# The end of round 0 spread over three engines in a fused RWKV-6 and MLP kernel

## The chip, the core and the metric

The kernel runs on one core of one Trainium2 chip. The core has TensorE (PE in the profile; its weight loads are listed apart as PEld), VectorE (DVE), ScalarE (ACT), GpSimd (POOL) and SyncE (SP), which here only issues transfers. Each runs its own instruction stream in order, and they meet through semaphores. The metric is the device time of one execution in microseconds (us). Five runs of the kernel before took 597.77, 600.28, 598.0, 605.68 and 603.4 us; their median is 600.28.

## The reference

Two blocks follow each other. The first is a linear attention with a state that decays per step; B, H, S, D are 4, 8, 768, 48:

```python
for t in range(S):
    kt, vt, rt, wt = (k[:, :, t], v[:, :, t], r[:, :, t], w[:, :, t])
    cur = np.einsum('bhd,bhe->bhde', u[None] * kt, vt)
    y[:, :, t] = np.einsum('bhd,bhde->bhe', rt, state + cur)
    state = wt[:, :, :, None] * state + np.einsum('bhd,bhe->bhde', kt, vt)
```

Its output, (4, 768, 8 x 48 = 384), is x for the second, a normalised two-layer MLP with a residual, of inner width 1536:

```python
xn = (x - mu) / np.sqrt(var + 1e-06) * g_ln
ch = np.maximum(xn @ w_ch1, 0.0) @ w_ch2
return (x + ch).astype(np.float32)
```

r, k, v, w and u come as float32. The two MLP weight matrices are float64 in the inputs.

## The kernel before

**Rounds and units.** The sequence of each of the 4 batches is cut into two halves of 384 steps. That makes 8 rounds, and each round has two units of 4 heads (`units`, q in the code; u0 and u1 are those of round 0, `new` those of round 1). A unit's 384 steps are 3 tiles of 128 rows, each of two chunks of 64 steps.

**One round of attention.** `load` brings w, k, r of a unit; `turned` transposes one pair of heads on PE (three 128x128 transposes into one of two PSUM buffers, tag "t") and ScalarE copies it out as wT, rT or kT. Inside a chunk, the scores are built in 6 levels by doubling blocks: `quads` multiplies kT and rT on PE into `a_ps` (one of two PSUM buffers of tag "a"), `grow` multiplies decays into rT and kT in place on VectorE, `keep` copies the level's part of the scores to A under a mask on VectorE. `totals` makes the decay products that the levels need. The last level isn't copied under a mask but as four blocks of 32 rows, together with four copies of rT to the other half of the partitions (`rx`, two per unit); `keep` only lists these eight copies and `finish(n)` does the next n of them, all on ScalarE. `ends` transposes the grown kT back (kn), `states` multiplies kn and v on PE (kv, tag "a") and runs the decayed sum over six chunks on VectorE (s), `exchanged` copies s to the other half of the partitions on ScalarE (sx). `outputs` multiplies A with v and vx (v with its chunk rows exchanged by a DMA) and rT, rx with s, sx into y (tag "a"), and VectorE adds the step's own term. That term, `own_term` (vo), is v times `own`, and `own` in rounds 0 and 1 comes from `products` (r times k on VectorE) and `product_sums` (12 records of own_ps on PE and a copy on ScalarE).

**The MLP of a round.** `moments` and `norm` normalise x (VectorE, one root on ScalarE), `turned_x` transposes it, `mlp` is a generator: 12 steps h (three 128x384 matmuls each, six records, then a copy with a floor at zero on ScalarE), then 12 steps of three matmuls of the second layer (o_ps). Its steps fill PE during the levels of the next round; `UNTIL` says how many steps are done when a level ends.

**Weights.** The float64 weights come in 24 parts of 128x384. `fetch` loads the next raw part (4 buffers, on SP's queue), `begin` splits it into three pieces with three ScalarE instructions and fetches another, `join` puts them together with three VectorE instructions (w_sb). The first 12 parts are the first layer's, the others the second's; from part 16 on a begin needs one of 4 small buffers, which the join four parts back frees. `converted(n)` joins up to part n just before an MLP step that needs it. `BEGINS` and `JOINS` set how many of each stand in the six levels of round 1.

**Order.** `InOrder` wraps every engine, so each engine's stream is the order of the code; the profile puts all its instructions on that wrapper's line 49, and they are told apart by tile names. SP's loads by `SPO` are in that order too. `fill` mixes a level's list of tasks (loads, begins, joins, round 2's transposes in `ahead`) with MLP steps. `warm(n)` puts multiplications of zeros by zeros, n blocks of 128 columns (tile idle), on PE.

**Around the change.** In round 0 there is no MLP yet. Its levels 2 to 5 each run three of the twelve transposes of round 1 (line 691 on). After level 5 come ends, round 1's products, finish, states, outputs, moments, norm and turned_x, and then the loop of rounds 1 to 8 (line 748 on).

Of the kernel before, what the change touches and what calls it, by code (L numbers as in the profile page):

```python
# [9 lines left out]
F32 = mybir.dt.float32  # L10
# [42 lines left out]
def kernel(  # L53
# [59 lines left out]
        for nm in "wkr"  # L113
    }
    vn, vx, xs = {}, {}, {}

    def steps(src, q, c):

# [309 lines left out]
                for j in range(2):  # L428
                    late.append((a["rx"][ds(HP * (1 - j), HP)], R[ds(HP * j, HP), :, 1, :]))

    def finish(n):

        for _ in range(n):
            out_, in_ = late.pop(0)
            ACT.copy(out=out_, in_=in_)

    def ends(q, pr):

# [45 lines left out]
                in_=a["s"].rearrange("p r (c i) e -> p r c i e", i=2)[ds(HP * j, HP), :, :, 0],  # L484
            )

    def outputs(q):
        b, f, g = units[q]
        a = st.pop(q)
        if g == 0:  # L490
            xs[b, f] = p2.tile([P, TT, H, D], F32, tag="x", name=f"x{b}_{f}")
        y = ps_a.tile([P, 2, 512], F32, tag="a", name=f"y{q}")
        y = y[:, :, 0 : NK * D].rearrange("p j (k e) -> p j k e", k=NK)
        A = a_bufs[q // U % 2]
        for k_ in range(NK):
            pr, c = divmod(k_, TT)
            for i in range(2):
                for j in range(2):
                    rows = ds(C * (i ^ j), C)
                    PE.matmul(  # L500
                        y[ds(C * i, C), j, k_], A[rows, j, q % U, k_, :],
                        vx[q][rows, c, pr] if j else vn[q][rows, c, 2 * pr],
                        start=k_ == 0, stop=False, skip_group_check=True,
                    )
# [15 lines left out]
        for j in range(2):  # L520
            DVE.tensor_tensor(
                out=xs[b, f][:, :, ts(g, NH)]
                .rearrange("p c (r j) e -> p j r c e", j=2)[:, j],
                in0=y[:, j].rearrange("p (r c) e -> p r c e", r=NP),
                in1=a["vo"].rearrange("p c (r j) e -> p j r c e", j=2)[:, j], op=ALU.add,
            )
        del vn[q], vx[q]


    xns, xTs, mvs = {}, {}, {}  # L530

    def moments(rnd):
        b, f = rounds[rnd]
        x, name = xs[b, f], f"{b}_{f}"
        stats = p2.tile([P, TT, DVE.BN_STATS_DIM], F32, tag="stats", name=f"stats{name}")
        mv = mvs[rnd] = p2.tile([P, TT, DVE.BN_AGGR_DIM], F32, tag="mv", name=f"mv{name}")
        for i in range(TT):
            DVE.bn_stats(out=stats[:, i, :], in_=x[:, i].rearrange("p h d -> p (h d)"))
        for i in range(TT):
            DVE.bn_aggr(out=mv[:, i, :], in_=stats[:, i, :])  # L540

    def norm(rnd):
        b, f = rounds[rnd]
# [137 lines left out]
    products(u1)  # L681
    quads(u1, 0)
    fetch(2)
    load(new[1], eng=SPO)
    run(each(load_v, [u0, u1], [SPO]) + each(load_vx, [u0, u1], [SPO]))
    begin()
    begin()
    warm(3)
    grow(u1, 0)
    keep(0, 0)  # L690
    ahead = each(turned, new[:1], "wrk", pairs) + each(turned, new[1:], "wrk", pairs)
    for lev in range(1, NLEV):
# [51 lines left out]
    while len(UNTIL) < NR * NLEV:  # L744
        UNTIL.append(UNTIL[-1] + MLP_STEPS // NLEV)
    ahead = [t for nm in "wkr" for t in each(turned, units_of(2), nm, pairs)]
    JOINS, BEGINS = (3, 3, 3, 4, 4, 4), (3, 3, 3, 3, 4, 2)
    for rnd in range(1, NR + 1):
        old, now, new = units_of(rnd - 1), units_of(rnd), units_of(rnd + 1)
        if rnd == 1:  # L750
# [1 line left out]
        for lev in range(NLEV):  # L752
# [123 lines left out]
```

## Time and profile before

| | before |
|---|---|
| median of 5 runs | 600.28 us (597.77 to 605.68) |
| the profiled execution | 597.77 us, its span 596.0 us |
| busy PE / VectorE / ScalarE / GpSimd | 574.5 / 295.1 / 198.1 / 70.6 us |
| mean granted TensorE clock | 0.982 |
| granted clock 42.6 to 59.6 us | 0.50 |
| grow of round 1's level 0 starts (VectorE) | 58.85 us |
| states of round 1 start (VectorE) | 112.52 us |

The span runs from the first to the last instruction of one profiled execution. The page gives each engine's busy time, then the span in 40 slices of 14.9 us with the busy share in tenths; "PEclk" is the share of full speed that TensorE's clock was granted. A busy PE isn't PE at full rate: a matmul's row counts from its issue to its modelled end, and neighbours overlap. A timeline row reads: start, duration, engine, line, operation, output and inputs, shape, count and, in brackets, the idle time before it and who ended it. A row of the chain of work reads: start, length, what.

### The profile page before, as it was taken

To read this page: it belongs to the slowest core of one execution; us is meant where nothing else is said; L and a number is where in the kernel's file an instruction comes from. 1 tells how busy PE (TensorE), PEld (TensorE's weight loads), DVE (VectorE), ACT (ScalarE), POOL (GpSimd) and SP (SyncE) were. 2 spreads that over 40 slices of the span, in tenths; PEclk is the share of its full clock that TensorE was granted. 3 is DMA by queue.
4 is the path that set the end of the run, shared out by engine and by line. 5 is a ranking of instruction groups with operands and counts; after the bars stand their busy time and mean duration, and the time that the engine had idled before them with its cause. 6 is when DMAs were issued, how large, how long until landed. Compare 5 with 4: busy or idle time off the path is not lost.

```text
span 596.0 us, 19117 instructions
## 1 busy us (share of the span) xinstructions
PE 574.5 (96%) x8542; PEld 387.7 (65%) x8542; DVE 295.1 (50%) x706; ACT 198.1 (33%) x430; POOL 70.6 (12%) x100
## 2 busy tenths in 40 slices
PE   8989997999999999999999999999999999999997
PEld 5679665666666666666666666667666666666554
DVE  4876997889365445425265334626245532130000
ACT  3483877503452125211343114321251015301200
POOL 6000000004250025000240007000230000000000
PEclk9995999999999999989999999999999999999999
DMA  9974896045323402222113402012000000000000
GB/s 146 201 187 111 177 252 164 3 89 115 62 43 70 99 15 41 55 58 59 30 26 63 95 14 55 2 32 58 15 2 3 15 25 5 2 14 26 0 14 26
DMA packets 122129, 36.82 MB, mean 62 GB/s; under 512 B 115776, under 2 KB 118976, under 8 KB 122048
## 3 DMA queue, kind: packets, MB, share of 16 engines
q1 hardware_dynamic: 119648, 35.31, 27.1%
q8 instruction: 67, 1.10, 0.8%
q10 hardware_dynamic: 2400, 0.30, 0.5%
q14 instruction: 14, 0.11, 0.1%
HBM read 28.51 MB, written 4.72 MB: 56 GB/s over the span
## 4 chain that ended last, share of the span: by engine, by line
PE 83%; DVE 10%; ACT 3%; issue 2%; POOL 1%; DMA 1%; DVEq 0%; POOLq 0%
PE o_ps L49 29%; PE h_ps L49 28%; PE a_ps L49 10%; PE y L49 4%; DVE w_sb L49 3%; DVE A L49 2%; PE kv L49 2%; PE r_ps L49 2%; PE k_ps L49 2%; DVE rT L49 2%; PE own_ps L49 1%; PE kn_ps L49 1%; PE w_ps L49 1%; PE xT_ps L49 1%; DVE kT L49 1%
## 5 line engine op out<-in xcount | busy, mean ns | idle before, releaser
L49 PE MATMUL o_ps<-w_sb,h 128*128 128x384 f32 x576 | 198.9, 492 | 3.2 <-ACT h L49 3.2
L49 PE MATMUL h_ps<-xT,w_sb 128*128 128x384 f32 x576 | 195.8, 489 | 0.6 <-ACT h L49 0.6
L49 PEld LDWEIGHTS o_ps<-w_sb,h 128*128 128x128 f32 x576 | 105.3, 191 | 65.2 <-ACT h L49 3.8
L49 PEld LDWEIGHTS h_ps<-xT,w_sb 128*128 128x128 f32 x576 | 105.4, 190 | 64.1 <-ACT h L49 0.8
L49 PEld LDWEIGHTS a_ps<-rT,kT 48*64 48x64 f32 x4608 | 74.7, 136 | 21.3 <-issue 13.4
L49 PE MATMUL a_ps<-rT,kT 48*64 48x32 f32 x4608 | 79.9, 221 | 5.8 <-issue 4.8
L49 ACT ACTIVATE h<-h_ps 128x384 f32<-128x384 f32 x96 | 46.5, 488 | 114.5 <-PE h_ps L49 110.2
L49 DVE TENSOR_TENSOR o<-o_ps,x 128x384 f32<-128x384 f32 x24 | 13.4, 558 | 133.1 <-PE o_ps L49 133.0
L49 POOL TENSOR_TENSOR vo<-v,own 128x576 f32<-128x576 f32 x12 | 14.3, 1195 | 363.0 <-DVE own L49 361.5
L49 DVE COPY_PREDICATED A<-mask,a_ps 128x384 f32<-128x384 int8 x80 | 54.6, 753 | 0.0
L49 DVE TENSOR_TENSOR kT<-kT,tot 128x384 f32<-128x384 f32 x80 | 45.5, 569 | 11.1 <-PE a_ps L49 10.3
L49 DVE TENSOR_TENSOR rT<-rT,tot 128x384 f32<-128x384 f32 x80 | 45.7, 580 | 8.7 <-PE a_ps L49 8.7
L49 DVE SCALAR_TENSOR_TENSOR s<-s,decay,kv 128x48 f32<-128x48 f32 x160 | 29.3, 260 | 28.1 <-PE kv L49 28.1
L49 DVE TENSOR_TENSOR x<-y,vo 128x288 f32<-128x288 f32 x32 | 13.2, 454 | 53.7 <-PE y L49 53.7
L49 ACT ACTIVATE xT<-xT_ps,g_sb 128x384 f32<-128x384 f32 x24 | 13.7, 581 | 59.8 <-PE xT_ps L49 59.8
L49 ACT COPY kT<-k_ps 128x384 f32<-128x384 f32 x32 | 14.9, 478 | 40.9 <-PE k_ps L49 40.9
L49 PEld LDWEIGHTS y<-v,A 64*64 64x64 f32 x384 | 22.9, 144 | 8.0 <-issue 6.0
L49 ACT COPY rT<-r_ps 128x384 f32<-128x384 f32 x32 | 14.4, 478 | 39.2 <-PE r_ps L49 39.2
L49 PE MATMUL y<-v,A 64*64 64x48 f32 x384 | 26.2, 232 | 0.8 <-DVE A L49 0.8
L49 PE MATMUL y<-vx,A 64*64 64x48 f32 x384 | 26.1, 232 | 0.0
L49 PE MATMUL y<-sx,rx 48*64 48x48 f32 x384 | 25.4, 229 | 0.0
L49 ACT COPY kn<-kn_ps 128x384 f32<-128x384 f32 x32 | 14.2, 481 | 30.3 <-PE kn_ps L49 30.3
(70 smaller groups left out, 554.0 us busy)
## 6 DMA issues: line engine op xcount, KB each, us to landing
raw<-in_moe_w_ch_dram SPq DMA_DIRECT2D x24, 384.0 KB, 4.3
nat_w<-in_w_dram SPq DMA_DIRECT2D x48, 96.0 KB, 2.8
nat_k<-in_k_dram SPq DMA_DIRECT2D x48, 96.0 KB, 3.0
v<-in_v_dram SPq DMA_DIRECT2D x48, 96.0 KB, 3.2
out_dram<-o SPq DMA_DIRECT2D x24, 192.0 KB, 1.9
nat_r<-in_r_dram SPq DMA_DIRECT2D x45, 96.0 KB, 2.9
vx<-v SPq DMA_DIRECT2D x32, 72.0 KB, 2.3
nat_r<-in_r_dram ACTq DMA_DIRECT2D x3, 96.0 KB, 4.0
```

Of the source, the lines that this page charges most:

```text
L49: return lambda *args, **kw: self.tc.keep_in_program_order(f(*args, **kw))
```

## The change

Four of the eight copies of `finish` go to VectorE and two to GpSimd. Both own terms of round 0 go to GpSimd. The products and sums of round 1's units are moved: those of its first unit between the outputs, those of the second behind them, its sums into round 1's level 0. The last output of round 0 is multiplied tile by tile, and its add on VectorE is split into six, each pair followed by that tile's moments. Round 1's transposes run as 2, 3, 3, 2, 2 in levels 1 to 5 instead of 3 in each of levels 2 to 5. One more begin runs in round 0's levels and one at the end of its tail; two are moved ahead of the loads of k and v. The numbers of warm blocks and the tables of MLP steps, joins and begins change. The diff, cut to its core:

```diff
-    def finish(n):
+    def finish(n, eng=ACT):
         for _ in range(n):
             out_, in_ = late.pop(0)
-            ACT.copy(out=out_, in_=in_)
+            (ACT.copy if eng is ACT else eng.tensor_copy)(out=out_, in_=in_)
...
-    def outputs(q):
+    def outputs(q, by_tile=False):
...
-        for k_ in range(NK):
-            pr, c = divmod(k_, TT)
+        order = [(pr, c) for pr in pairs for c in range(TT)]
+        if by_tile:
+            order.sort(key=lambda at: at[1])
+        for pr, c in order:
+            k_ = pr * TT + c
...
-        for j in range(2):
-            DVE.tensor_tensor(
...
+        for cs in [[c] for c in range(TT)] if by_tile else [range(TT)]:
+            c, n = cs[0], len(cs)
+            for j in range(2):
+                DVE.tensor_tensor(
...
+            if by_tile:
+                moments(q // U, c, 1)
...
-    load(new[1], eng=SPO)
-    run(each(load_v, [u0, u1], [SPO]) + each(load_vx, [u0, u1], [SPO]))
+    load(new[1], "wr", SPO)
     begin()
     begin()
+    load(new[1], "k", SPO)
+    run(each(load_v, [u0, u1], [SPO]) + each(load_vx, [u0, u1], [SPO]))
...
-        if lev > 1:
-            run(ahead[3 * lev - 6 : 3 * lev - 3])
-        if lev in (3, 4):
+        run(ahead[(0, 2, 5, 8, 10)[lev - 1] : (2, 5, 8, 10, 12)[lev - 1]])
+        if 1 < lev < NLEV - 1:
             begin()
-        warm((6, 3, 2, 2, 3)[lev - 1])
+        warm((3, 1, 1, 2, 0)[lev - 1])
...
     run(each(ends, [u0, u1], pairs))
-    for q in new:
-        products(q)
-    finish(6)
-    warm(1)
+    finish(4, DVE)
+    finish(2)
+    finish(2, POOL)
     states(u0)
     exchanged(u0)
-    finish(2)
+    own_term(u0, POOL)
     states(u1)
+    product_sums(u1)
+    own_term(u1, POOL)
     exchanged(u1)
-    product_sums(u1)
     load(units_of(2)[0], "w", SPO)
-    own_term(u0, DVE)
+    warm(2)
+    products(new[0])
+    outputs(u0)
+    warm(3)
     begin()
-    outputs(u0)
-    product_sums(new[0])
-    begin()
-    own_term(u1, DVE)
     join()
-    outputs(u1)
-    product_sums(new[1])
-    moments(0)
+    outputs(u1, by_tile=True)
+    warm(2)
     load(units_of(2)[1], "w", SPO)
     for q in new:
         quads(q, 0)
+    products(new[1])
+    product_sums(new[0])
     norm(0)
     begin()
     join()
     warm(2)
     run(each(turned_x, [0], range(KC)))
+    begin()
     join()
...
-    UNTIL = [3, 6, 8, 11, 14, 16, 19, 21, 24]
+    UNTIL = [4, 7, 10, 12, 14, 16, 19, 21, 24]
...
-    JOINS, BEGINS = (3, 3, 3, 4, 4, 4), (3, 3, 3, 3, 4, 2)
+    JOINS, BEGINS = (3, 3, 4, 4, 4, 3), (3, 3, 3, 4, 4, 2)
...
+                if lev == 0:
+                    tasks += each(product_sums, now[1:])
```

More of the change, by code (lines that the diff above doesn't have):

```diff
@@ L115 @@
     vn, vx, xs = {}, {}, {}
+    xns, xTs, stats, mvs = {}, {}, {}, {}
     def steps(src, q, c):
@@ L502, in outputs @@
                         vx[q][rows, c, pr] if j else vn[q][rows, c, 2 * pr],
-                        start=k_ == 0, stop=False, skip_group_check=True,
+                        start=(pr, c) == order[0], stop=False, skip_group_check=True,
                     )
@@ L519, in outputs, with moments @@
                     )
-        for j in range(2):
-            DVE.tensor_tensor(
[L522 to L526, printed above, removed]
+        for cs in [[c] for c in range(TT)] if by_tile else [range(TT)]:
+            c, n = cs[0], len(cs)
+            for j in range(2):
+                DVE.tensor_tensor(
+                    out=xs[b, f][:, ds(c, n), ts(g, NH)]
+                    .rearrange("p c (r j) e -> p j r c e", j=2)[:, j],
+                    in0=y[:, j].rearrange("p (r c) e -> p r c e", r=NP)[:, :, ds(c, n)],
+                    in1=a["vo"][:, ds(c, n)].rearrange("p c (r j) e -> p j r c e", j=2)[:, j],
+                    op=ALU.add,
+                )
+            if by_tile:
+                moments(q // U, c, 1)
         del vn[q], vx[q]
-    xns, xTs, mvs = {}, {}, {}
-    def moments(rnd):
+    def moments(rnd, at=0, n=TT):
         b, f = rounds[rnd]
         x, name = xs[b, f], f"{b}_{f}"
[L535 to L540, printed above, removed]
+        if at == 0:
+            stats[rnd] = p2.tile([P, TT, DVE.BN_STATS_DIM], F32, tag="stats", name=f"stats{name}")
+            mvs[rnd] = p2.tile([P, TT, DVE.BN_AGGR_DIM], F32, tag="mv", name=f"mv{name}")
+        for i in range(at, at + n):
+            DVE.bn_stats(out=stats[rnd][:, i, :], in_=x[:, i].rearrange("p h d -> p (h d)"))
+        for i in range(at, at + n):
+            DVE.bn_aggr(out=mvs[rnd][:, i, :], in_=stats[rnd][:, i, :])
     def norm(rnd):
```

## The prediction

> **What bounds the kernel now.** I read the page's slices first, then its busy rows by stretch, the chain of work that ended last, and the timeline of each engine. In the slices (40 of 14.9 us each) PE stands at 9 nearly everywhere, and its granted clock dips in the fourth, 45 to 60 us:
>
> ```profile
> PE   8989997999999999999999999999999999999997
> ...
> DVE  4876997889365445425265334626245532130000
> ...
> PEclk9995999999999999989999999999999999999999
> ```
>
> From about 135 us on PE works through the MLP without much pause, and the change leaves that stretch alone. What the change is worth is therefore how much sooner round 2's level 0 begins. Before it, VectorE and TensorE pace each other. Busy time by stretch (after PE, PEld, DVE, ACT and POOL: granted clock, DMA share, GB/s):
>
> ```profile
> 36.00:39.20 3.20, 2.96 (x53) 2.21 (x54) 1.88 (x5) 2.37 (x6) 0.00 (x0) 1.00 0.50 81
> 39.20:42.60 3.40, 2.10 (x84) 1.92 (x76) 2.81 (x17) 3.30 (x8) 0.00 (x0) 1.00 1.00 365
> 42.60:59.60 17.00, 17.00 (x310) 16.07 (x309) 11.70 (x35) 7.92 (x19) 0.00 (x0) 0.50 0.50 127
> ...
> 97.20:100.60 3.40, 1.64 (x5) 1.06 (x6) 3.02 (x9) 3.19 (x7) 0.00 (x0) 1.00 0.83 198
> ```
>
> At the end of round 0 the clock is halved for 17 us, though PE is "busy" throughout: its work there is the thin kind (outputs y, sums own_ps, quads a_ps). VectorE is idle for 5.3 of those 17 us, GpSimd for all. The chain that ended last runs through PE at that clock:
>
> ```profile
> 39.03 0.36 ACT A L49
> ...
> 40.88 0.92 PE kv L49 x48
> 41.80 1.92 PE own_ps L49 x12
> 43.72 2.75 PE y L49 x88
> 46.46 2.65 PE own_ps L49 x12
> 49.11 2.75 PE y L49 x88
> 51.86 2.66 PE own_ps L49 x12
> ...
> 55.15 1.26 DVE xn L49 x3
> ```
>
> At full clock the same chain has "122.53 1.79 PE y L49 x93" and "12.31 1.30 PE own_ps L49 x12". So both outputs and all three sums of this stretch wait on each other at half speed, and norm's root (54.71) waits for the last sum. Round 1's level 0 starts on VectorE at 58.85 (the timeline; the chain has 58.93). In round 1 VectorE is near full to 92 us, and the waits that count are these, from ScalarE's, PE's and VectorE's timelines:
>
> ```profile
> 97.35 1.22 ACT L49 ACTIVATE rest<-raw 128x384 int32<-128x384 uint32 x2 [1.62 <-DVE w_sb L49]
> ```
> ```profile
> 98.96 3.49 PE L49 MATMUL o_ps<-w_sb,h 128*128 128x384 f32 x10 [3.15 <-ACT h L49]
> ```
> ```profile
> 103.35 1.26 DVE L49 TENSOR_TENSOR kT<-kT,tot 128x384 f32<-128x384 f32 x2 [1.95 <-PE a_ps L49]
> ```
>
> The last first-layer copy h queues on ScalarE behind a weight split that waits for a join; PE then waits 3.15 us for h, and VectorE 1.95 us for PE.
>
> **The change, part by part.** Levels 1 to 5 of round 0. The quads of levels 3, 4, 5 start 3.56 us apart (25.72, 29.28, 32.84). In that chain a level is quads 1.53 + a transpose group 0.49 + ScalarE's copy that frees the buffer 0.49 + the third group 0.55 + warm 0.44. Level 1, bound by VectorE, takes two groups free. Levels 4 and 5 lose the third group and the wait before it, levels 2, 3 and 5 lose warm work. VectorE's floor in a level is four grows and a keep, 4 x 0.47 + 0.95 = 2.8. I take 0.4 (level 2), 0.2 (level 3), 0.5 (level 4): -1.1, between 0 (VectorE is the bound already) and -2.0 (every level at the floor).
>
> The tail, 32.84 to 58.85 in before, laid out anew from 31.7. Level 5's quads end at 33.2; two transpose groups instead of three and no warm, so the four kn groups run 34.3 to 36.2. finish(4) on VectorE: no such copy in the trace; bounds are the 0.20 of a 128x48 copy and the 0.75 of a 128x384 predicated one; I take ScalarE's 0.47 for the same shape, 4 x 0.47 = 1.9, done by 36.4. That is VectorE time in which it waited before (1.76 us ahead of the states), and it frees the score buffer for kv of u1, which PE waited 1.3 us for. rx of u1 on GpSimd: 0.22 (its 64x32 mask copy) to 0.83 (its 128x384 product) each; 0.8, as nearest in size, is needed only 7 us later. own_term on GpSimd 1.15 to 1.66 each (rows at 139.6 and 142.7) instead of 0.75 on VectorE: also hidden, vo of u0 by 37.2, of u1 by 41.5. kv 36.2 to 38.0, states on VectorE 37.2 to 41.3 (2 x 2.05), own_ps of u1 38.0 to 39.3, sx 40.2, y of u0 from 40.2. Products of new[0] 0.94 on VectorE after the states, its sums off the path between the outputs.
>
> The clock: I expect it to fall again near 42, since kv, sums and y are the same, and to come back sooner, because warm(2), warm(3), warm(2) are now among them. One output at half (2.75), warm(3) at about 1.3 (the 256-column warm took 1.22 for two records at half against 0.60), one at 1.64 (88 of the 93 in 1.79): y of u1 ends near 46. VectorE adds u0's output (0.82), joins (1.27) and then goes by tiles: six adds of 96 columns, between a 128x48 update's 0.18 and 128x288's 0.41, say 0.23, so 1.4 instead of 0.82; with moments 3 x 1.03, ending 48.3; products of new[1] 49.2. PE's quads and own_ps of new[0] end at 49.3 at full clock, 51.8 at half; the root waits for the sum as before. Then recip, xn 1.4 and two joins 2.6: level 0 at 53.3 to 56.0 on VectorE; I take 54.2.
>
> DMA adds to this. The two splits' fetches (384 KB each) now stand on SP's queue ahead of new[1]'s k, all v and vx. DMA share was 0.9 to 1.4 from 16 to 26 us, at some 200 GB/s, so 2 x 384 KB is up to 3.9 us; with the slack after 30 us (0.34 to 0.80) about 3. v of u1 landed near 35.6 (vx, which reads it, was issued then) and would land near 38.6, when kv of u1 could start at 37.1; k of new[1] is needed at 33.2. Cost 0 to 3, taken 0.3 after the waits already there. Level 0 is at 54.5: -4.4 including the levels.
>
> Round 1. In the new order, h3 is the last step of level 0 and needs join 6, the last of that level; h6 likewise needs join 9. The last third of such a step (0.65, of h's 1.94 per six records) and the first unit's quads (0.80) now stand between VectorE's last join and its next grow: +1.6 after level 0, +1.6 after level 1, about +0.4 after level 2, where join 13 covers it. In return the first layer is done a level sooner and the last split is in level 4 instead of behind the copies of level 5. These VectorE waits go: 0.67 (92.4), 1.95 (103.4), 1.0 (0.62 and 0.38 at 110.9 and 112.1): -3.6. Next late are PE's kn transposes, the two MLP steps (6 x 0.65 = 3.9) and kv behind the grown kT: 6.8 against VectorE's 6.75 of grows, own term and three joins. PE also idles ahead of them, which can pull its clock down: 0 to 1.8, taken 1.2. product_sums of new[1], 1.3 at full clock, moves into level 0, where PE waits for join 6 anyway. Sum of round 1: 1.6 + 1.6 + 0.4 - 3.6 + 1.2 = +1.2, between -0.4 and +3.
>
> In all -4.4 + 1.2 = -3.2 us. The profiled execution has 597.77, its span 596.0 and 1.7 around it; so 594.5 for one like it. The median of the runs shown is 2.5 higher, so 597.0.
>
> The Trainium skill speaks at two places. "TensorE: Matmul & The Clock Gate", Part 1, has the clock fall after an idle window of about 3.4 us and rise after a busy one; the 17 busy us at 0.50 disagree unless thin work isn't counted. By that rule the warm calls would be needless, and level 0 would come at full clock, the second rival's sum. "VectorE: DVE Perf Modes", Rules for kernel authors, says to keep the number of operations small; by it the tiles are a plain loss of 0.6 us, where my sum has that loss hidden while y comes at half speed.
>
> **Rivals.** Second: the clock holds or returns within one window of 3.4 us, level 0 at 53 and PE's round 1 unslowed: -5.5 to -6.5, 594. For it: more warm between outputs; against it: kv and sums fill a window as in 39.2 to 42.6. Third: the gain is lost to PE waiting for fresh joins and to late v; each at its dear end (+3 in round 1, +1.5 from DMA), no change, 600. Fourth, slower: nine of 16 warm blocks in levels 1 to 5 are gone, and the clock falls already in level 4. The point: the stretch 97.2 to 100.6 kept it with 1.64 us of wide matmuls; levels 4 and 5 have 0.66 of transposes and 0.44 or no warm besides quads. Price: quads 2.79 for 1.53 in two levels (2.5), kn transposes 1.1, kv 1.4, sums 1.3 (each about doubled, as quads and sums are), all 6.3 against 4.4 won, and 1.2 from round 1: +3.1, 603.4. Against it: each level keeps two or three transpose groups, and level 1 gains two.
>
> **Numbers.** Forecast 0.50, second 0.22, third 0.16, fourth 0.12. About 1%, 6 us, is what a measurement of this kernel can tell from no change. Range 590 to 604: the second's far end less the runs' scatter, up to the fourth. Faster by over 1% is most of the second and an edge of the forecast, 0.26; slower an edge of the fourth and what I haven't seen, 0.10; within 0.64.
>
> **What would show it.** Level 0's first grow on VectorE near 54.5 instead of 58.85; a half-clock stretch of 3.4 to 10 us instead of 17; in round 1 VectorE waiting 1.6 us twice for PE after the joins of levels 0 and 1; no 3.15 us wait of o_ps for h; round 2's states on VectorE near 109.3 instead of 112.5. Wrong if the clock falls before kn, if kv waits for v by more than 1 us, or if GpSimd's copies run past 40 us.

## The result, and the profile after

The changed kernel takes 603.13 us in the median, the kernel before, on the same chips, 600.28. The ratio is 1.0063, with a 95% interval of 1.0049 to 1.0078: **slower by 0.6%**, where the forecast was 3.2 us less. The profiled execution took 600.09 us with a span of 598.4, against 597.77 and 596.0.

The page of the kernel after, three rows of its slices (PE's busy tenths, VectorE's, and the granted clock):

```profile
PE   8998998999999999998999999999999999999997
...
DVE  4887678879545455435255434626245532130000
...
PEclk9996898999999999999999999999999999999999
```

The dip in the clock is still there, in the fourth and fifth slice, and a new one follows in the seventh. Busy time by stretch, with the columns of the same view of before (PE, PEld, DVE, ACT, POOL, granted clock, DMA share, GB/s):

```profile
36.00:39.20 3.20, 3.01 (x107) 2.48 (x106) 2.84 (x10) 2.74 (x6) 2.16 (x3) 1.00 0.33 63
39.20:42.60 3.40, 3.40 (x103) 3.06 (x102) 3.40 (x21) 1.25 (x4) 1.15 (x1) 1.00 0.42 67
42.60:59.60 17.00, 14.66 (x228) 11.81 (x223) 12.62 (x35) 7.35 (x16) 0.00 (x0) 0.67 0.54 148
48.27:65.34 17.07, 16.92 (x142) 12.92 (x137) 14.69 (x38) 6.71 (x15) 0.00 (x0) 0.50 0.49 98
97.20:100.60 3.40, 1.41 (x15) 0.76 (x8) 3.23 (x8) 3.34 (x9) 0.00 (x0) 0.83 0.44 72
99.50:106.30 6.80, 6.12 (x10) 3.19 (x10) 6.29 (x15) 5.23 (x11) 0.00 (x0) 0.50 0.72 206
```

Up to 42.6 us the change does what it should: VectorE and PE are full, PE's wait ahead of kv is gone, GpSimd works. But the stretch at half clock is as long as before, 17.07 us, only 5.7 us later, so that it now reaches into round 1's first MLP steps. Late in round 1 a second one follows, from 99.47 to 106.30 us; the kernel before kept the full clock there. The chain that ended last shows what lies in it (start, length, what):

```profile
43.57 1.43 PE y L49 x80
44.99 2.19 issue
47.18 0.33 PE y L49 x8
47.51 0.63 PE idle L49 x2
48.14 2.59 PE a_ps L49 x96
50.74 2.66 PE own_ps L49 x12
53.40 0.02 issue
53.42 0.17 ACT own L49
53.59 0.20 ACT rstd L49
...
54.03 0.49 DVE xn L49
...
59.86 4.05 PE h_ps L49 x6
```

Three things stand here that before's chain doesn't have. PE pauses for 2.19 us, eight records before the end of the second output, with no wait that the profile shows ("issue"). The quads and the sums of new[0], both at half clock, then stand ahead of norm's root, because ScalarE copies the sums (own) before it takes the root (rstd); VectorE had the moments ready at 51.12. And the first MLP step takes 4.05 us, where a step at full clock takes 1.94.

VectorE's waits after the joins of levels 0, 1 and 2, and PE's wait for the last first-layer copy (timelines):

```profile
72.04 0.56 DVE L49 TENSOR_TENSOR rT<-rT,tot 128x384 f32<-128x384 f32 x1 [4.28 <-PE a_ps L49]
81.66 0.56 DVE L49 TENSOR_TENSOR rT<-rT,tot 128x384 f32<-128x384 f32 x1 [1.87 <-PE a_ps L49]
90.51 0.56 DVE L49 TENSOR_TENSOR rT<-rT,tot 128x384 f32<-128x384 f32 x1 [0.50 <-PE a_ps L49]
```
```profile
100.18 6.51 PE L49 MATMUL o_ps<-w_sb,h 128*128 128x384 f32 x10 [1.99 <-ACT h L49]
```

The ten records of the last row lie in that second stretch: they take 6.51 us where the same ten took 3.49 before.

| | before | after |
|---|---|---|
| kv of u0 starts | 38.67 | 37.53 |
| second output ends | 51.86 | 47.51 |
| xn starts | 55.15 | 54.03 |
| level 0 starts on VectorE | 58.85 | 57.73 |
| first MLP step starts | 60.07 | 59.72 |
| states of round 1 (VectorE) | 112.52 | 115.11 |
| span less PE's busy time | 21.5 | 22.6 |

Of 4.35 us gained at the second output 1.1 are left at level 0 and 0.35 at the first MLP step. PE is busy 96% of both spans, so the span can also be read from PE: its idle time rose by 1.1 us, and the mean clock, 0.982 before and 0.980 after, costs by estimate (1 - 0.982) x 596.0 = 10.7 and (1 - 0.980) x 598.4 = 12.0 us; together these are about the 2.4 us between the spans.

### The profile page after: what moved, and what is told of

Its sections match the earlier page's. It is cut to its first block, busy times and chain, and to the rows that moved or that the text cites. A ratio compares the mean times of both kernels' runs of the same rounds, so it can differ in the third digit from the quotient of the medians.

```text
span 598.4 us, 19130 instructions
## 1 busy us (share of the span) xinstructions
PE 575.8 (96%) x8542; PEld 386.2 (65%) x8542; DVE 296.2 (50%) x712; ACT 196.0 (33%) x424; POOL 74.2 (12%) x104
## 4 chain that ended last, share of the span: by engine, by line
PE 88%; DVE 4%; ACT 3%; DMA 2%; issue 2%; SPq 1%; ACTq 0%; DVEq 0%
PE h_ps L49 31%; PE o_ps L49 29%; PE a_ps L49 11%; PE y L49 4%; PE kv L49 2%; PE k_ps L49 2%; PE xT_ps L49 2%; PE kn_ps L49 2%; PE r_ps L49 2%; PE w_ps L49 2%; PE own_ps L49 1%; PE idle L49 1%; DMA nat_r<-in_r_dram 1%; ACT rest L49 1%; DVE A L49 1%
## 5 line engine op out<-in xcount | busy, mean ns | idle before, releaser
L49 PE MATMUL h_ps<-xT,w_sb 128*128 128x384 f32 x576 | 198.3, 493 | 0.4 <-DVE w_sb L49 0.4
L49 POOL TENSOR_TENSOR vo<-v,own 128x576 f32<-128x576 f32 x14 | 16.7, 1190 | 336.8 <-DVE own L49 332.3
L49 DVE SCALAR_TENSOR_TENSOR s<-s,decay,kv 128x48 f32<-128x48 f32 x160 | 29.3, 259 | 28.7 <-PE kv L49 28.7
L49 DVE TENSOR_TENSOR x<-y,vo 128x288 f32<-128x288 f32 (+1 forms) x36 | 13.5, 418 | 51.7 <-PE y L49 51.7
L49 ACT ACTIVATE xT<-xT_ps,g_sb 128x384 f32<-128x384 f32 x24 | 13.7, 581 | 58.1 <-PE xT_ps L49 58.1
L49 PEld LDWEIGHTS y<-v,A 64*64 64x64 f32 x384 | 21.0, 133 | 8.3 <-issue 6.9
L49 PE MATMUL y<-v,A 64*64 64x48 f32 x384 | 24.0, 222 | 0.3 <-DVE A L49 0.3
L49 PE MATMUL y<-vx,A 64*64 64x48 f32 x384 | 23.9, 222 | 0.0
L49 ACT COPY kn<-kn_ps 128x384 f32<-128x384 f32 x32 | 14.2, 481 | 28.7 <-PE kn_ps L49 28.7
L49 PE MATMUL y<-sx,rx 48*64 48x48 f32 x384 | 23.4, 218 | 0.0
```

The lines of the kernel that those rows point to most:

```text
L49: return lambda *args, **kw: self.tc.keep_in_program_order(f(*args, **kw))
```

## The experiments

All ratios are to the kernel before on the same chip, from 12 runs of each kernel (6 of e3, over 40 of the kernel after). The clock is the mean granted clock over all timed runs of a kernel, not only the profiled one; the kernel before has 0.979. The last column is the start of the first MLP step in the profile (us). Each kernel has one profile, and its half-clock stretches are one draw; the ratios rest on more.

| kernel | ratio (95%) | clock | first step |
|---|---|---|---|
| after | 1.0063 (1.0049 to 1.0078) | 0.979 | 59.72 |
| e1 after, old tables | 1.0046 (1.0020 to 1.0071) | 0.979 | 60.44 |
| e2 after, more zero work | 1.0007 (0.9977 to 1.0038) | 0.989 | 57.81 |
| e3 after, old order of loads | 1.0145 (1.0101 to 1.0188) | 0.973 | 64.48 |
| e4 before, new tables | 1.0010 (0.9981 to 1.0039) | 0.979 | 60.56 |
| e5 e2, old tables | 1.0003 (0.9966 to 1.0040) | 0.990 | 60.51 |
| e6 e2, root first | 0.9975 (0.9937 to 1.0013) | 0.991 | 58.17 |
| e7 before, more zero work | 1.0010 (0.9968 to 1.0053) | 0.987 | 56.59 |
| e9 e2, w loaded later | 0.9995 (0.9956 to 1.0034) | 0.992 | 57.18 |
| e10 new order of the tail | 0.9973 (0.9939 to 1.0008) | 0.988 | 58.74 |
| e11 e10 by tiles | 0.9987 (0.9957 to 1.0017) | 0.987 | 56.25 |
| e12 e10, old tables | 0.9999 (0.9957 to 1.0041) | 0.984 | 56.07 |
| e13 after, root first | 1.0015 (0.9986 to 1.0044) | 0.982 | 58.00 |
| e14 after, sums between outputs | 1.0040 (1.0008 to 1.0073) | 0.979 | 59.10 |
| e15 root, sums, loads, one piece | 0.9994 (0.9962 to 1.0026) | 0.984 | 54.76 |
| e16 e15, 5 blocks more | 0.9985 (0.9952 to 1.0018) | 0.988 | 59.25 |
| e17 e15 without the spread | 1.0081 (1.0047 to 1.0115) | 0.975 | 64.63 |
| e18 pause filled, 15 blocks | 0.9985 (0.9945 to 1.0025) | 0.987 | 54.45 |
| e19 pause filled, 21 blocks | **0.9927 (0.9885 to 0.9970)** | 0.989 | 54.95 |

### The tables of steps, joins and begins (e1, e4, e5, e12)

First theory: the new tables, which put fresh joins ahead of MLP steps, cost what the change wins. e1 puts the old ones into the kernel after, e4 the new ones into the kernel before.

```diff
-    UNTIL = [4, 7, 10, 12, 14, 16, 19, 21, 24]
+    UNTIL = [3, 6, 8, 11, 14, 16, 19, 21, 24]
-    JOINS, BEGINS = (3, 3, 4, 4, 4, 3), (3, 3, 3, 4, 4, 2)
+    JOINS, BEGINS = (3, 3, 3, 4, 4, 4), (3, 3, 3, 3, 4, 2)
```

> The changed kernel with the old tables of MLP steps, joins and begins in round 1. Two theories of the 0.6% loss. Joins: the first-layer steps that now wait for the level's last join cost it (VectorE waits 4.28 and 1.87 us after levels 0 and 1 in the changed kernel's trace, none in the old one's); without them the tail's 1.1 us and the waits of levels 4 and 5 decide, ratio to before 0.996 to 1.000, no wait of VectorE for quads over 1 us after levels 0 and 1. Clock: the half-clock stretch is as long as before (17.07 us) but now lies over the second unit's sums and the first layer's first steps, so PE is late whatever the tables; ratio 1.003 to 1.006, VectorE still waits 2 us or more after level 0.

> The kernel before with the three new tables alone (MLP steps, joins, begins of round 1), everything else as before. Joins: VectorE waits 1.6 us after levels 0 and 1 and 0.4 after level 2, and saves up to 3.6 us of waits in levels 3 to 5: 1.000 to 1.005. Clock: the tables alone do no harm since PE is at full speed from 59.6 us on: 0.995 to 1.001.

e1's interval overlaps that of the kernel after: the old tables aren't shown to win the loss back. In its profile a wait of 3.63 us stands again late in round 1. e4 isn't told apart from the kernel before; VectorE waits 1.87, 1.87 and 0.51 us there too, and the later waits are gone. e5 is the same trial at a held clock (e2 below with the old tables), e12 with the new order of the tail (e10 below).

> The kernel after with the three tables of before (steps, joins, begins) and with the extra zero work that kept the clock up (which alone gave a ratio of 1.0007 to before and waits of VectorE of 1.87, 1.87 and 0.51 us after levels 0 to 2). Theory joins (the new tables cost what they bring and more): these three waits shrink together by 2.5 us or more, the last split stands again ahead of a first-layer copy late in round 1 (a wait of 2 to 3.6 us there), and the ratio falls to 0.995 to 0.998 only if that late wait is under 2. Theory neutral tables (what the fresh joins cost, the earlier split gives back, as the tables put alone into the kernel before gave 1.001): ratio 0.999 to 1.003, waits moved but their sum in round 1 within 1 us of 4.25.

> The same new order of the tail with the tables of steps, joins and begins of before. Theory PE's account: VectorE's waits of 1.87, 1.87 and 0.5 go, but PE's wait of 3.15 for the last first-layer copy stands again in the place of 1.99, and 0.95 ahead of round 2; PE's idle time in round 1 rises by 1 to 2 us and the ratio by 0.001 to 0.003. Theory joins: the ratio falls by 0.003 or more (4.2 us of waits gone).

e5 isn't told apart from e2, nor e12 from e10. In e12 the waits after the joins are under 0.7 us, and one line takes their place (VectorE's timeline):

```profile
102.72 1.26 DVE L49 TENSOR_TENSOR kT<-kT,tot 128x384 f32<-128x384 f32 x2 [4.90 <-PE a_ps L49]
```

What follows: in four settings no effect of the tables stands clear of the intervals (the four ratios move by -0.0017, +0.0010, -0.0004 and +0.0026), and the theory that the joins make the loss isn't borne out. Where VectorE waits 1.87 us "<-PE a_ps", PE is busy with MLP steps that have to be done at some time; such a wait moves work, and loses none while PE works on.

### The clock (e2, e7)

e2 adds 16 blocks of zero work behind the second output of the kernel after, so that the clock doesn't fall there. e7 adds 17 to the tail of the kernel before. The edit of e2:

```diff
     outputs(u1, by_tile=True)
-    warm(2)
+    warm(9)
...
         quads(q, 0)
+    warm(3)
     products(new[1])
     product_sums(new[0])
+    warm(6)
```

> The changed kernel with more warm blocks in the tail: 9 instead of 2 after the last output, 3 more after the quads, 6 more after the sums (16 in all, about 2.6 us of PE time, of which some 1.5 us delay the sums). Clock: the half-clock stretch shrinks to 7 us or less, the first h step starts near 56 instead of 59.9, ratio to before 0.993 to 0.998. Joins: the clock may be held, but the waits after levels 0 and 1 stay at 1.6 us each or more and the time stays at 1.003 to 1.007.

> The kernel before with extra zero work in its tail alone: warm(2) ahead of the first output, 3 after it, 3 after the second, 6 after the last sums, 3 after the quads. Theory clock (the half-clock stretch of 17 us in the tail is what holds up level 0): the stretch is gone or under 7 us, the two outputs and three sums take 1.8 and 1.3 us each, y of u1 ends near 48 instead of 51.86, level 0 starts near 55.8 instead of 58.85, ratio 0.994 to 0.996. Theory covered (VectorE and ScalarE are next late, and the zero work itself takes the time): level 0 within 1 us of 58.85, ratio 0.999 to 1.001.

e2's profile has no half clock before 97 us, and the ratio falls by 0.0056, 3.4 us; its interval lies clear of that of the kernel after. The ratio still lies between the ranges of the two theories, and the first MLP step starts at 57.81, not near 56. e7's profile also holds the clock (1.00 from 42.6 to 59.6) and level 0 starts at 55.79, as the theory of the clock asked, but the ratio is 1.001: its clock, 0.987 on the mean of its runs, is worth about 0.008 x 600 = 4.6 us, and 17 blocks at 0.25 (2.21 us for nine in e2) cost 4.2. By this estimate the zero work costs about what it wins there. It can pay only where PE would have stood idle or where it prevents more half clock than it costs.

### The loads (e3, e9)

e3 puts the two added splits behind the loads of k, v and vx again.

```diff
-    load(new[1], "wr", SPO)
-    begin()
-    begin()
-    load(new[1], "k", SPO)
+    load(new[1], eng=SPO)
     run(each(load_v, [u0, u1], [SPO]) + each(load_vx, [u0, u1], [SPO]))
+    begin()
+    begin()
```

> The changed kernel with the two begins (and their 384 KB fetches) behind the loads of k, v and vx again, as before. If late v or the crowded DMA queue at 40 to 45 us (PE pauses 2.19 us inside the last output at 45.0, waiting for nothing that the profile shows) is part of the loss: that pause goes and the time falls by 1 to 2 us, ratio 1.003 to 1.005. If not: 1.005 to 1.008. Both other theories expect no more than 0.2% from it.

None of the theories had this one. ScalarE's timeline:

```profile
40.54 0.54 ACT L49 ACTIVATE w_sb<-raw 128x384 f32<-128x384 f32 x1 [7.23 <-DMA raw<-in_moe_w_ch_dram]
```

With one begin more in the levels, that of level 4 needs a raw part that is here fetched late; the copies behind it on ScalarE, and PE behind them, wait 7 us, and kv starts at 45.50. The fetches ahead of k and v are thus a condition of the added begin, not an edit by itself. My fear for v wasn't borne out: v of u1 landed at 37.72 in the kernel after and kv didn't wait for it.

e9 takes the kernel of e2 and loads w of round 2's first unit behind the second output, to see whether PE's pause follows the transfers.

```diff
-    load(units_of(2)[0], "w", SPO)
     warm(2)
...
+    load(units_of(2)[0], "w", SPO)
     load(units_of(2)[1], "w", SPO)
```

> The kernel after with the extra zero work and with the first load of w for round 2 moved behind the second output, beside the other. Theory transfers (PE's pause of 2.1 us among the last records of y of u1, for which the profile shows no wait, is PE's own instructions arriving late while transfers run at 300 to 400 GB/s): with 384 KB less in that stretch the pause falls by 0.5 us or more, y of u1 ends at 46.8 or sooner instead of 47.3. Theory place (it belongs to that place in PE's stream, whatever the transfers): the pause stays at 2.0 to 2.2 at the same record. Either way the root's wait for the sums covers it in part: ratio 0.999 to 1.001.

The pause fell to 1.36 us and the second output ended at 46.63, as the theory of transfers had it. But e10, which has the same late load, has 2.18 us again (next part), so that the late load alone doesn't shorten the pause.

### Root, order and tiles (e13, e6, e10, e11)

e13 is the smallest edit: norm moves up by two lines. e6 is the same on top of e2.

```diff
-    products(new[1])
-    product_sums(new[0])
     norm(0)
+    products(new[1])
+    product_sums(new[0])
```

> The kernel after with one step moved: norm's root ahead of the products of new[1] and the sums of new[0]. No zero work is added. Theory root: the reciprocal starts near 51.7 instead of 53.82, and the first MLP step 1 us or more sooner than 59.72; the ratio falls from 1.0063 to 1.003 to 1.005. Theory clock alone: PE at half speed is late for the transposes of xn anyway (its sums end near 53.4), the first MLP step within 0.5 us of 59.72 and the ratio 1.0055 to 1.007.

> The kernel after with the extra zero work, and with norm's root issued ahead of the products of new[1] and the sums of new[0], so that ScalarE's root no longer stands behind the copy of these sums. Theory root (the tail's gain was lost because the root waits on ScalarE for a copy that waits for PE's sums, with the moments done 2.5 us before): the wait of the reciprocal of 1.66 us falls to under 0.6, xn starts near 51.2 instead of 53.66, level 0 near 55.7 instead of 57.35, states of round 1 near 112.4 instead of 114.05, ratio 0.997 to 0.998. Theory hidden (round 1 is bound by PE and by the joins, and level 0's start is not what counts): level 0 earlier, but the waits after it grow by as much, states near 114, ratio 1.000 to 1.002.

ScalarE's timeline in e13:

```profile
50.73 0.30 ACT L49 ACTIVATE rstd<-mv,eps 128x3 f32<-128x3 f32 x1 [6.01 <-DVE mv L49]
52.44 0.17 ACT L49 COPY own<-own_ps 128x12 f32<-128x12 f32 x1 [1.42 <-PE own_ps L49]
```

The root now waits for VectorE's moments (mv) and no longer for the copy; xn starts at 51.27 instead of 54.03, the first MLP step 1.72 us sooner, and the ratio falls by 0.0048, 2.9 us, of a loss of 3.8 us. Its interval and that of the kernel after don't meet. The mean clock of its runs is higher too, 0.982 against 0.979, by the estimate above some 2 of these 2.9 us; what the shorter path gives without the clock wasn't separated. e6, with the clock held as well, has 0.9975; the reciprocal's wait falls from 1.66 to 0.36 and the states of round 1 start at 111.69, as expected or sooner.

e10 also puts the last output in one piece, moves the products of new[1] ahead of it, their sums from level 0 into the tail and both loads of w behind the output; e11 is e10 by tiles.

```diff
-    outputs(u1, by_tile=True)
+    products(new[1])
+    outputs(u1)
+    moments(0)
...
+    norm(0)
+    warm(2)
     product_sums(new[0])
-    norm(0)
+    warm(2)
+    product_sums(new[1])
```

> The kernel after with its tail put in another order: both loads of w behind the second output, the products of new[1] ahead of that output's adds, that output in one piece (not by tiles), norm's root ahead of both sums, the sums of new[1] in the tail again, zero work of 2 blocks three times there (11 blocks instead of 9). Theory PE's account (the time is PE's useful work plus its idle time, its zero work and half of what it runs at half clock; VectorE's waits beside a busy PE cost nothing): y of u1 ends near 46.7, xn starts near 50.2 instead of 54.03, the first step of the MLP near 54 instead of 59.72, PE idles 1 to 2 us less before level 0; ratio 0.993 to 0.997 if no stretch of 17 us at half clock follows, 0.999 to 1.002 if one does. Theory joins (VectorE's waits for fresh joins in round 1 are what counts): these stay at 1.87, 1.87 and 0.5, so the ratio stays at 1.000 or above.

> The same new order of the tail with the last output by tiles as in the kernel after. Theory tiles cost (the first tile's add waits for the last record of y all the same, so 3.46 us of adds and moments stand after it instead of 2.6): the add starts within 0.3 us after y's end, xn 0.8 to 0.9 us later than in one piece, ratio 0.001 to 0.0015 higher. Theory tiles overlap: the first add starts at least 0.4 us before y's end, and xn is no later.

e10 has 0.9973, just above the range expected with a held clock; its profile shows 10.2 us at half from 49.5 on. Its second output has a pause of 2.18 us, from 45.23 to 47.41 (stretches of e10, same columns as above):

```profile
45.00:46.00 1.00, 0.23 (x10) 0.10 (x4) 0.96 (x3) 0.11 (x1) 0.00 (x0) 1.00 0.08 19
46.00:47.40 1.40, 0.00 (x0) 0.00 (x0) 0.68 (x2) 0.00 (x0) 0.00 (x0) 1.00 0.73 185
```

In the first of the two, DMA moves 19 GB/s and PE stands still all the same. So transfers at that moment aren't what PE waits for.

By tiles, the first of the six adds in e11 starts at 48.69, 0.14 us after y's end at 48.55, though that tile's own records were done long before (in the kernel after: 47.65 against 47.51). So nothing overlaps, and from y's end to xn it is 4.18 us by tiles and 3.26 in one piece. The ratios differ by 0.0014, as expected in size, but the intervals overlap.

### PE's pause (e14, e15, e16)

The page's list of DMA queues has the row

```profile
q8 instruction: 67, 1.10, 0.8%
```

which is 1.10 MB for PE's 8542 matmuls and as many weight loads, 64 bytes each; a packet is 16 KB, so 256 of them. One output is 96 of each, 192 instructions in some 1.8 us. In the kernels with a pause a packet of q8 starts at 44.1 to 47.0 us, and PE goes on 2.2 to 2.5 us after that start (2.8 in e1), however long the pause. In all their traces it comes behind the same number of PE's matmuls, 982 in the trace from the start of the program, whatever instruction stands there. The kernel after has another such pause, of 0.56 us, behind 602, inside the quads of round 0's level 5; 380 matmuls lie between the two, and three packets hold 384 pairs of a matmul and its weight load. e14 puts the sums, few instructions in 1.3 us, between the two outputs again, with nothing else changed but that the root is free by it.

```diff
     outputs(u0)
     warm(3)
+    product_sums(new[0])
...
     products(new[1])
-    product_sums(new[0])
     norm(0)
```

> The kernel after with one step moved back: the sums of new[0] stand between the two outputs, as before. Theory supply (PE's pause of 2.1 us comes because two outputs back to back use up PE's instructions faster than the next lot arrives; in nine kernels PE went on 2.2 to 2.5 us after the packet that fetched the lot): the sums, 24 short records in 1.3 us, fill that time, the pause falls to under 1.0 us, y of u1 ends at 48.0 or sooner though 1.3 us of sums come first, the root no longer waits for a copy (reciprocal near 51.7 instead of 53.82), ratio 1.000 to 1.003. Theory transfers (the pause follows the weights' transfers at 300 to 400 GB/s): the pause stays at 1.9 or more, y of u1 ends near 48.8, ratio 1.003 to 1.006.

The chain of e14:

```profile
44.56 1.23 PE own_ps L49 x12
45.80 1.20 PE y L49 x68
46.99 0.93 issue
```

The pause falls from 2.19 to 0.93, by as much as the sums take. And it moves: it comes behind 68 records of y where it came behind 80 in the kernel after, 12 sooner for the 12 records of the sums put in ahead. The pause stands at a place counted in PE's instructions, which fits the end of a packet; the reading is that PE waits for the next one, and that the sums give that one time to come. The time didn't follow as expected, though: y ended at 48.80, since kv started 1.0 us later in this profile, the clock fell for 17.1 us again, and the ratio of 1.004 isn't told apart from that of the kernel after. e15 joins this with the root first, the one piece and the late loads; e16 adds 3 blocks ahead of the quads and 2 behind them.

```diff
     warm(3)
+    product_sums(new[0])
...
-    outputs(u1, by_tile=True)
-    warm(2)
+    products(new[1])
+    outputs(u1)
+    moments(0)
...
-    products(new[1])
-    product_sums(new[0])
     norm(0)
+    warm(4)
...
-    warm(2)
```

> The kernel after with the sums of new[0] between the outputs, both loads of w behind the second, the products of new[1] ahead of its adds, that output in one piece, the root first, and 4 blocks of zero work after the quads (9 blocks in the tail, as in the kernel after). Theory PE's account: no pause of over 1 us in the tail, y of u1 ends near 48, xn near 51, the first MLP step near 54.5 at full clock; ratio 0.990 to 0.995 if the clock holds to level 0, 0.997 to 1.000 if it falls. Theory joins: the waits of VectorE in round 1 stay at 1.87, 1.87 and 0.5, ratio 0.999 or above.

> The same with 3 blocks of zero work ahead of the quads and 6 after them (14 blocks). Theory clock: 1.5 us more of zero work, in time in which PE waits for xn anyway, keeps the clock up; half-clock time in the tail and level 0 under 4 us, mean granted clock over 0.990, ratio 0.990 to 0.994, lower than with 9 blocks. Theory zero work costs (it delays the transposes of xn by as much as it wins): ratio within 0.001 of that with 9 blocks or higher.

e15's profile has no pause and its first MLP step at 54.76, but the clock falls at 53.7, and the ratio is 0.9994, at the end that I had given for a fallen clock. e16 isn't told apart from it; in its profile the pause, 1.48 us, is back and the clock falls before it is over, at 47.4 us, ahead of the 5 blocks. Up to the end of the second output the two have the same instructions on PE, and yet one pauses and the other doesn't: e15's packet starts at 43.83, e16's at 45.63. e15's weight parts were issued 1.4 to 2.1 us sooner (38.66, 39.31, 40.50 against 40.80, 41.46, 41.94), and its DMA share from 44 to 45 us is 0.13 against 1.05. So the transfers may well hold up the packet, and with it PE; that wasn't tried by itself. What follows: place and timing say that PE waits for its instructions, what delays them stays open, and a shorter pause didn't pay by itself where the clock fell all the same.

### The spread over engines (e17)

e17 is e15 with all finish copies on ScalarE and both own terms on VectorE, as before.

```diff
-    finish(4, DVE)
-    finish(2)
-    finish(2, POOL)
+    finish(6)
     states(u0)
     exchanged(u0)
-    own_term(u0, POOL)
+    finish(2)
...
-    own_term(u1, POOL)
+    own_term(u0, DVE)
+    own_term(u1, DVE)
```

> The same as with 9 blocks, but the finish copies all on ScalarE and both own terms on VectorE, as before. Theory spread helps: PE waits 1.3 us again for a copy ahead of kv of u1, VectorE has 1.5 us more to do between the states and the second output's adds; xn 1 to 1.5 us later, ratio 0.002 to 0.003 higher. Theory spread is hidden: ratio within 0.001.

The ratio rises by 0.0087, 5.2 us, three to four times what I had expected, and the intervals of e15 and e17 don't meet. PE's timeline, and a stretch with the usual columns:

```profile
42.20 1.46 PE L49 MATMUL kv<-v,kn 64*64 64x48 f32 x48 [1.53 <-ACT A L49]
```
```profile
42.30:62.80 20.50, 20.47 (x359) 17.94 (x360) 13.34 (x43) 8.03 (x19) 0.00 (x0) 0.50 0.37 100
```

PE's wait for ScalarE's finish copies is back, and right behind it the clock falls for 20.5 us. The wait is 1.53 us; most of the price is the clock, whose mean over the runs falls from 0.984 to 0.975, by the same estimate some 5 us. **The spread itself is a gain**, most of it a clock that isn't lost. (e17's profile has 6.83 us at half clock from 28.7 us on too, ahead of its edit, so that it is a draw.)

### Together (e18, e19)

e18 adds zero work to e15 where PE would stand still: 4 blocks behind the sums between the outputs (the pause) and 6 ahead of the transposes of xn; the sums of new[1] move to level 1. e19 has 7 and 9 blocks; the cut shows it against e15.

```diff
     product_sums(new[0])
+    warm(7)
     begin()
...
     norm(0)
-    warm(4)
+    warm(9)
...
-                if lev == 0:
+                if lev == 1:
                     tasks += each(product_sums, now[1:])
```

> The kernel with the sums of new[0] between the outputs and the root first (one piece, loads of w late), with 4 blocks of zero work behind these sums, 6 ahead of the transposes of xn, and the sums of new[1] put into round 1's level 1 instead of ahead of the first MLP step (15 blocks in the tail). Theory place of the clock (half clock costs most where wide matrix work stands: 1.9 us of loss per MLP step pair, little where thin work stands; zero work costs nothing where PE would pause for its instructions or for xn): the pause in the second output falls under 0.6 us, the first MLP step stands near 54.5 at full clock, half-clock time before 65 us under 4; ratio 0.992 to 0.996. Theory zero work costs: y of u1 ends 1.2 us later, the pause goes but the first MLP step stands at 56 or later; ratio 0.998 to 1.001.

> The same with 7 blocks behind these sums and 9 ahead of the transposes (21 blocks). Theory place of the clock: the further 1.9 us are only worth it if the 15 blocks let the clock fall; if they hold it, the ratio rises by 0.002 to 0.003. Theory zero work costs: ratio higher by 0.003.

In e19 nothing is at half clock before 64.9 us, and the second output has only a trace of the pause, 0.11 us, now behind 62 records of y, 6 sooner than in e14 for the 6 records of zero work (its chain):

```profile
45.49 1.63 PE idle L49 x6
47.11 1.19 PE y L49 x62
48.30 0.11 issue
48.41 0.62 PE y L49 x23
```

e19's ratio is 0.9927, its interval wholly below 1: it beats both kernels, the one after by 1.4%. Its mean clock, 0.989 against 0.979, is by the estimate above worth some 6 us. It is the best of 18 variants, which favours it somewhat. My expectation that the further 6 blocks cost 0.002 to 0.003 was a miss, but e18, at 0.9985, isn't told apart from e19, so their order stays open. e18 is a miss of its own: its profile has what the first theory asked (a pause of 0.08 us, the first MLP step at 54.45, no half clock before 64 us), but its ratio lies in the range of the other. VectorE still waits 2.93, 2.38 and 0.50 us after the joins in e19, more than in e2: once more, those waits aren't what counts. But in both kernels PE itself now waits for a join ahead of an MLP step (e18's timeline; 2.01 us in e19), and the clock falls behind it, at 64.2 and 64.9 us:

```profile
63.11 0.88 PE L49 MATMUL h_ps<-xT,w_sb 128*128 128x384 f32 x2 [2.02 <-DVE w_sb L49]
```

With the tail this short, fresh joins do cost PE time, so the four pairs above don't clear the tables here.

## Why the prediction was wrong

The time measured lies inside the range, and within 1% of before, but the forecast of a gain was wrong. By its steps:

- **Levels, -1.1: wrong, nothing was won there.** VectorE's first grow of level 5 starts at the same time, before and then after:

```profile
33.81 1.26 DVE L49 TENSOR_TENSOR kT<-kT,tot 128x384 f32<-128x384 f32 x2 [0.64 <-PE a_ps L49]
```
```profile
33.84 1.26 DVE L49 TENSOR_TENSOR kT<-kT,tot 128x384 f32<-128x384 f32 x2 [0.68 <-PE a_ps L49]
```

  Level 4's quads start at 29.28 in both. Level 5's start 0.8 us sooner, at 32.05, but PE then stands still, for nothing that the profile shows (PE's timeline, after):

```profile
33.04 1.47 PE L49 MATMUL a_ps<-rT,kT 48*64 48x32 f32 x82 [0.56 <-issue]
```

  The 1.14 us by which kv starts sooner come behind level 5, where a transpose group and warm work are gone; the sum had both gains, kv at 36.2, and kv came at 37.53.
- **Tail, -4.4 with the levels: wrong, -1.1 was measured.** The gain was there at the second output (-4.35) and was lost behind it. Two terms failed. First, y of u1 was to end near 46 and ended at 47.51: kv came 1.3 us late and PE paused for 2.19, which I didn't have, and the full clock up to there, which the sum hadn't assumed, gave back part. I read the sums between the outputs as work that stood in the way; by e14 they also gave PE's instructions time to come. Second, "the root waits for the sum as before" was right, but I put level 0 between a full and a half clock (54.2 between 53.3 and 56.0), and half clock came: quads 2.59 and sums 2.66. With the 1.5 us by which y was late on top of 56.0 one is at 57.5; 57.73 was measured. The sum should have asked whether a root that waits for a sum has to stand there at all: e13 gives back three quarters of the loss by moving it up, part of that through the clock. (88 of 93 records in 1.79 us are 1.69, not 1.64; that slip changes nothing.)
- **Clock, "fall again near 42 and come back sooner", 3.4 to 10 us: wrong.** It fell at 48.3 and stayed for 17.07 us. The change removed PE's wait of 1.30 us ahead of kv, behind which it fell before (e17 puts it back, and the clock falls there), and the pause took its place. In the 3.41 us ahead of the fall PE was busy 2.1 us before, 1.22 after.
- **The small prices** held: a finish copy 0.56 on VectorE (taken 0.47), rx 0.53 on GpSimd (0.8), own term 1.15 (1.15 to 1.66), a tile's add 0.21 (0.23), DMA hidden. But "the loss of the tiles is hidden while y comes at half speed" was wrong: all adds wait for the whole of y, and the tiles lengthen the path by 0.9 us (e11).
- **Round 1, +1.2: wrong, 2.59 + 1.12 = +3.7 was measured at the states.** The waits after the joins were 4.28, 1.87 and 0.50 where I had 1.6, 1.6 and 0.4; the excess after level 0 lies where the half clock and the sums that moved there are, which no run separates. Those of 0.67, 1.95 and 1.0 went, as predicted; PE's 3.15 shrank to 1.99 instead of vanishing, and behind it the clock fell for 6.83 us, where I had put a slower PE at 1.2, at most 1.8: ten records alone took 3.0 us more. The deeper error is the measure: I summed VectorE's waits as losses. In e4, e12 and e19 they come and go with no like change of the time, since PE works on meanwhile.

Of the rivals, the fourth (603.4) came nearest to 603.13, and that is luck: in the profile of the kernel after, levels 4 and 5 kept the full clock, and none of its four prices was paid; only its mechanism, a clock that falls where thin work is left alone, was seen, in the second output. Its own fall does occur: the profiles of e1 and e17, two of the 17 with the new levels, have 6.83 us at half clock from 30.0 and 28.7 us on, the three with the old levels none there. What it adds to the mean of the kernel after isn't known. The third (gain lost to joins and late v, 600) had no loss and causes that weren't borne out.

Stretches at half clock here are 3.41, 6.83, 10.2, 13.7, 17.07 and 20.5 us long, multiples of 3.41. The Trainium skill, "TensorE: Matmul & The Clock Gate", Part 1, has the clock fall after an idle window of some 3.4 us of a free-running grid. The lengths fit the grid; but PE was no more than partly idle in the window ahead. Two stretches side by side, e10 and then e6:

```profile
46.10:49.50 3.40, 2.09 (x106) 2.02 (x107) 2.16 (x6) 0.00 (x0) 0.00 (x0) 1.00 0.94 223
```
```profile
45.64:49.06 3.42, 1.65 (x12) 1.08 (x13) 1.21 (x6) 0.00 (x0) 0.00 (x0) 1.00 1.04 224
```

After the first, 106 records of y and quads in 2.09 us, the clock fell. After the second, 12 records in 1.65 us of which most is zero work of full width, it held. Busy time of thin records seems to count for less; that is a reading of such pairs, and in e7 a window (38.16 to 41.58) that was 2.12 us busy, most of it thin kv records, held as well. Where the border lies was not tried by itself.

What stays open: over all runs the kernel after has the same mean clock as the kernel before, 0.979, so the 1.3 us of clock in the profiled pair are no mean difference. At an equal clock of 0.98, straight lines give 600.1 before (29 runs) and 602.3 after (all its runs). Of these 2.2 us the profile names 1.1 as idle PE; the rest I can't place.

## What to carry to other kernels

Where one engine is busy 96% of the time, sum up that engine's idle time, its clock and its filler work, and read another engine's waits only as hints of order. A path that an edit shortens has to be followed to the next wait of every engine in order: here a copy queued ahead of a root on ScalarE ate much of the gain, and moving the root up gave back three quarters of the loss. Short records that seem to stand in the way can be what gives an instruction stream its time, and a pause of 2 us can cost several times that if the clock falls behind it (17.07 us at half clock here).

## What the runs showed of the hardware

- **Instruction supply.** Two outputs almost back to back, 384 instructions within some 4 us, seem to outrun the packets of 256: PE goes on 2.2 to 2.8 us after the packet's start, with no wait in the profile but "issue", always at the same place in its stream. 1.3 us of work with few instructions between them hid as much of it.
- **The scatter is the clock.** Over 29 runs of the kernel before, from 597 to 606 us, the time falls by 5.7 us per 0.01 of mean granted clock, with a correlation of -0.98; one us lost to the clock is about one us of time. A profile of one run says little of a kernel's mean clock: e7's had 0.996, the mean of its runs is 0.987.
- **GpSimd's copies** across the halves of the partitions took 0.53 us each for 64x384 float32, a third less than the 0.83 of its product of 128x384.
